# Attention and feed-forward in one kernel: w3 turned on TensorE as 32-bit words of two fp16 neighbours

## The chip, the cores and the metric

The kernel runs on one core of one Trainium2 chip. The metric is device time in microseconds (us) for one execution. The kernel before takes 422.37 us, the median of three runs (421.72 to 423.1).

## What is computed

The reference is attention with pooled queries, followed by a feed-forward block without an activation function:

```python
# q, k, v: (8, 8, 1152, 64); w1, w2: (512, 1024); w3: (1024, 1024); w_out: (1024, 512)
q_pool = q.reshape(B, H, S // 2, 2, D).mean(axis=3)          # 576 queries a head
scores = q_pool @ k.T / sqrt(D)
attn   = softmax(scores)
x      = (attn @ v), heads side by side                      # 4608 x 512
h      = (x @ w1) * (x @ w2) @ w3
out    = h @ w_out                                           # 4608 x 512, float32
```

All inputs are float32 in device memory; the kernel works in fp16 and accumulates in float32.

## The kernel before, in words

**Weights.** There is nothing between w3 and w_out but two products, so the kernel first forms T = w3 @ w_out (1024 x 512, `T16`) and later multiplies by T. For that it needs w3 with its columns on the partitions. `t_groups` (L466 to 493) does this. `turn(ft)` takes 128 rows of w3 (`w3c`, fp16, cast by the load) and turns them on TensorE with eight 128x128 transposes against `ident16` into one bank of PSUM (L475); VectorE copies the bank to `w3T` (L478). `mult(ft, n0)` then adds eight matmuls up (L484), with one 128x128 block of `w3T` as weights and a block of 256 columns of w_out (`wosb`) as moving operand, and VectorE casts the result into `T16` (L487). There are 8 turns and 16 such products of eight matmuls; the order is two turns, four products, and so on. `w3T` has two buffers.

**Attention.** Heads go in pairs, 32 pairs. A pair's k and q are loaded, cast to fp16 by GpSimd (L300 to 306) and transposed: on TensorE for the first eight pairs (`transp_pe`, L328, copied by VectorE at L330), by DMA afterwards. Scores are made in groups of 512 columns for both heads (L388) into one of three PSUM buffers (`psc`), and ScalarE's exponential moves each group into a ring in SBUF (L393). An AV group (`av_pair`, L413) multiplies 128 queries' worth of the ring by v, for both heads, into one PSUM bank (`avb`); VectorE takes reciprocals (L431), scales (L439) and, after a transpose on TensorE (L446 or L448), copies the result into `xT` (L455 or L457). The next AV group writes the same bank and waits for these.

**Feed-forward.** `xT` is worked off in nine chunks of 512 tokens (`moe_groups`): 16 projection groups of four (or eight) matmuls with w1 and w2 (L506), then four output groups of eight matmuls with `T16` (L550). VectorE (ScalarE, late in the kernel) takes them out of PSUM.

**Order.** All engines work off lists written in program order; a planner (`_Plan`) decides at build time what stands between the score groups on TensorE. The work is cut into 108 visits of three score groups each. After the scores of a visit, `plan.visit` tries sequences of fills (turns, products, projections, output groups, each into the bank `mo` or, as `mot`, into one of the three `psc` buffers), AV groups and pair transposes, and takes the one with the least lost time by its own costs: `STEP` for a fill of size n (0.45 us for a turn, n = 0.5), 0.69 us for the copy behind it, and so on. The T fills are offered from visit 3 on. A chunk of the feed-forward is offered when the AV groups that it needs are done. So a changed cost or size of one fill can move all that follows.

**Loads.** GpSimd's queue (software descriptors) brings w3 in four pieces (`w3_load`), w_out, w1, w2 and the pairs' k, q and v early on; SP's queue brings others. At the start GpSimd's list is: identity, casts of pair 0, w3 piece 0 (L607), w_out (L611), casts of pair 1, loads of pair 2, v of pair 1, cast of v of pair 0, w3 piece 1, loads of pair 3.

**The end.** `rzall` holds the reciprocals of the softmax sums. After the last AV group VectorE tests that each lies in a range, counts, and a matmul sums the count over the partitions (L744 to 757). If any test failed, a general path (`_general`) computes everything again from the inputs; otherwise it is skipped.

Of the kernel before, what the change touches and what calls it, by code (L numbers as in the profile page):

```python
# [8 lines left out]
FP32 = mybir.dt.float32  # L9
FP16 = mybir.dt.float16  # L10
AF = mybir.ActivationFunctionType
ALU = mybir.AluOpType


def _make_identity(nc, ident):
    nc.gpsimd.memset(ident, 0.0)
    nc.gpsimd.affine_select(
        out=ident, in_=ident, compare_op=ALU.not_equal, fill=1.0,
        base=0, channel_multiplier=1, pattern=[[-1, ident.shape[1]]],
    )  # L20
# [101 lines left out]
class _Plan:  # L122
# [1 line left out]


    SWITCH, SLOT, AV, TURN, PAIR, SEEN = 0.09, 0.222, 0.553, 0.055, 0.76, 0.05
    STEP = {0.5: 0.45, 1: 0.866, 2: 1.73}

    def __init__(self, t):
        self.t = t  # L130
# [21 lines left out]
    def fill(self, n, at, scored):  # L152
        b = self._psc() if scored else None
        self._pe(False, max(at, (self.psc[b] if scored else self.mo) + self.SEEN), self.STEP[n])
        self.dve = max(self.dve, self.t + 0.2) + 0.69
        if scored:
            self.psc[b] = self.dve + 0.07
        else:
            self.mo = self.dve + 0.07
# [58 lines left out]
def kernel(  # L218
# [11 lines left out]
    nc = tc.nc  # L230
# [7 lines left out]
    NF = dff // 128  # L238
# [16 lines left out]
    const = ctx.enter_context(tc.tile_pool(name="const", bufs=1))  # L255
# [4 lines left out]
    fast.enter_context(tc.manual_schedule())  # L260

    ident16 = const.tile([128, 128], FP16)
    vaugs = [const.tile([128, 2, NJ, E1], FP16, name=f"vaug{i}") for i in range(NVA)]
    rzall = const.tile([128, NU, 2], FP32)
    w1sb = wpool.tile([128, NC, dff], FP16)
    w2sb = wpool.tile([128, NC, dff], FP16)
    T16 = wpool.tile([128, NF, dm], FP16)
    msb = fast.enter_context(tc.tile_pool(name="m_sb", bufs=1))
    w3c = [msb.tile([128, 4, dff], FP16, tag="g8", bufs=2, name=f"w3c{i}") for i in range(2)]
    wosb = msb.tile([128, NF, dm], FP16)  # L270
    ring = att.tile([128, 2, RING], FP16, tag="ring", bufs=1)
    avb = ps.tile([128, 512], FP32, tag="av", bufs=1)
# [8 lines left out]
    def load_kq(p, k_eng, q_eng):  # L281
        b, h0 = p // HP, 2 * (p % HP)
        kst = att.tile([128, 2, NJ * D], FP32, tag="kst")
        k_eng.dma_start(out=kst, in_=k[b, h0:h0 + 2].rearrange("u (p c) d -> p u (c d)", p=128))
        qst = att.tile([128, 2, QM * 2 * D], FP32, tag="qst")
        qtl = att.tile([QT, 2, 2 * D], FP32, tag="qtl")
        q_eng.dma_start(out=qst, in_=q[b, h0:h0 + 2, 0:QM * 256].rearrange("u (p c) d -> p u (c d)", p=128))
        q_eng.dma_start(out=qtl, in_=q[b, h0:h0 + 2, QM * 256:S].rearrange("u (p t) d -> p u (t d)", t=2))
        kq[p] = (kst, qst, qtl)
# [7 lines left out]
    def cast_kq(p):  # L297
        kst, qst, qtl = kq.pop(p)
        kq16 = kq16s[p % 2]
        nc.gpsimd.tensor_copy(out=kq16[:, 0:NJ].rearrange("p c u d -> p u c d"),  # L300
                              in_=kst.rearrange("p u (c d) -> p u c d", d=D))
        qv = qst.rearrange("p u (c t d) -> p u c t d", t=2, d=D)
        eng = nc.gpsimd
        eng.tensor_tensor(out=kq16[:, NJ:NJ + QM].rearrange("p c u d -> p u c d"),  # L304
                          in0=qv[:, :, :, 0], in1=qv[:, :, :, 1], op=ALU.add)
        eng.tensor_tensor(out=kq16[0:QT, NJ + QM], in0=qtl[:, :, 0:D], in1=qtl[:, :, D:2 * D], op=ALU.add)
        pairs[p] = kq16
# [57 lines left out]
    def first_turn(c0, c1, pt, *engs):  # L365
        kq16, kqT = kq16s[0], pairs[0][2]
        for c in range(c0, c1):
            nc.tensor.transpose(pt[:, (c - c0) * 128:(c - c0) * 128 + 128],
                                kq16[:, c].rearrange("p u d -> p (u d)"), ident16)
        w = (c1 - c0) // len(engs)  # L370
        for n, eng in enumerate(engs):
            o = n * w
            eng(out=kqT[:, c0 + o:c0 + o + w].rearrange("p c i -> p (c i)"), in_=pt[:, o * 128:(o + w) * 128])

    def turn_bank():
        return ps.tile([128, 512], FP32, tag="mo", bufs=1, name="ptf").bitcast(FP16)
# [90 lines left out]
    def t_groups():  # L467
        w3T = {}

        def turn(ft):  # L470
            def go(pt):
                w3T[ft] = msb.tile([128, NF, 128], FP16, tag="w3T", bufs=2, name="w3T")
                ph = pt.bitcast(FP16)
                for a in range(NF):
                    nc.tensor.transpose(ph[:, a * 128:a * 128 + 128],  # L475
                                        w3c[ft // 4][:, ft % 4, a * 128:a * 128 + 128], ident16)

            return 0.5, go, lambda pt: nc.vector.tensor_copy(out=w3T[ft].rearrange("p a i -> p (a i)"),  # L478
                                                             in_=pt.bitcast(FP16)), W3_AT[ft // 2]

        def mult(ft, n0):
            def go(pT):
                for a in range(NF):
                    nc.tensor.matmul(pT[:, 0:256], w3T[ft][:, a, :], wosb[:, a, n0:n0 + 256],  # L484
                                     start=(a == 0), stop=(a == NF - 1))

            return 1, go, lambda pT: nc.vector.tensor_copy(out=T16[:, ft, n0:n0 + 256], in_=pT[:, 0:256]), WO_AT  # L487

        for ft in range(0, NF, 2):
            yield turn(ft)  # L490
            yield turn(ft + 1)
            for n in range(4):
                yield mult(ft + n // 2, n % 2 * 256)
# [116 lines left out]
    def w_load(dst, src):  # L610
        nc.gpsimd.dma_start(out=dst, in_=src.rearrange("(c p) f -> p c f", p=128))  # L611
# [11 lines left out]
    first_casts()  # L623
    rest_casts()
    w3_load(0)
    w_load(wosb, moe_w_out)
    cast_kq(1)
    load_kq(2, nc.gpsimd, nc.gpsimd)
    load_v(1, nc.gpsimd)
    cast_v(0)  # L630
# [50 lines left out]
            ready.append(held.pop(0)[1])  # L681

    NVIS = NS // VS
    seen, due, started = -1, 0.0, False
    for vis in range(NVIS):
        if vis == T_START:
            queue.append(t_groups())
        due = max(due + PACE, plan.t + 2.6)
        for s in range(vis * VS, vis * VS + VS):
            pn = (s * G + G - 1) // FLAT  # L690
            if pn != seen:
                seen = pn
                if pn == 0:
                    first_turn(0, K0, turn_bank(), nc.scalar.copy)
                    first_turn(NJ, NJ + QM, avb.bitcast(FP16), nc.vector.tensor_copy, nc.scalar.copy)
                if NPE <= pn + 1 < NP:
                    transp(pn + 1)
                if 0 < pn < NP - 2:
                    prepare(pn + 2)
                elif pn + 2 == NP:  # L700
                    cast_v(NP - 1)
            scores(s)
            plan.scores()
            if s == 0:
                first_turn(NB - 1, NB, turn_bank(), nc.vector.tensor_copy)
        if vis == 0:
            first_turn(K0, NJ, turn_bank(), nc.vector.tensor_copy)
            prepare(2)
        avail = NT5 * sum(1 for e in pair_end if e < vis) - avn[0]
        turn = [p for p in range(1, NPE) if (p * FLAT // G) // VS - 1 == vis]  # L710
        while ready:
            started = True
            queue.append(moe_groups(ready.pop(0)))
        head(4)

        must = sum(1 for i in range(avn[0], min(avn[0] + avail, NU))
                   if ((i // NT5 * NJ * Sq + RING + TO[i % NT5]) // G) // VS <= vis + 1)
        for what in plan.visit(due, [on_pe(avn[0] + j - 1) for j in range(avail)], must, [(g[0], g[3]) for g in ahead],
                               [KQ_AT.get(p, 0.0) for p in turn], 0.05 if started else 0.1):
            if what == "P":  # L720
                plan.pair(KQ_AT.get(turn[0], 0.0))
                transp_pe(turn.pop(0))
            elif what == "A":
                av_step()
                plan.av_group(on_pe(avn[0] - 2))
            else:
                fill(what == "s")
# [18 lines left out]
    nc.vector.tensor_tensor(out=ok[:, 0, :], in0=ok[:, 0, :], in1=ok[:, 1, :], op=ALU.mult)  # L746
    okn = const.tile([128, 1], FP32)
    nc.vector.reduce_sum(out=okn, in_=ok[:, 0, :], axis=mybir.AxisListType.X)
    okh = const.tile([128, 1], FP16)
    nc.vector.tensor_copy(out=okh, in_=okn)  # L750
    ones = const.tile([128, 1], FP16)
    nc.vector.memset(ones, 1.0)
    for _ in range(12):
        fill()
    nc.tensor.matmul(avb[0:1, 0:1], okh, ones, start=True, stop=True)
    badi = const.tile([1, 1], mybir.dt.int32)
    nc.vector.tensor_scalar(out=badi, in0=avb[0:1, 0:1], scalar1=-1.0, scalar2=float(128 * NQ),
                            op0=ALU.mult, op1=ALU.add)
    while not near[0]:
        fill()  # L760
    bad = nc.values_load(badi[0:1, 0:1], min_val=0, max_val=128 * NQ)
    while fill():
        pass
    fast.close()
# [32 lines left out]
```

## Time and profile before

| | |
|---|---|
| median of three runs | 422.37 us (421.72 to 423.1) |
| the profiled execution, its own time | 421.38 us |
| its span, first to last instruction | 419.4 us |
| TensorE busy | 406.3 us, 97% of the span |
| ScalarE busy | 326.4 us, 78% |
| VectorE busy | 204.8 us, 49% |
| GpSimd busy | 165.7 us, 40% |
| turns of w3 (L475) | 64 transposes, first at 18.1 us, last at 55.7 us |
| copies of the turns (L478) | 8, 0.69 us each |
| products (L484) | 128 matmuls, first at 21.4 us, last at 65.6 us |
| load of w_out | issued at 8.6 us, landed 11.2 us later |

In the profile, PE is TensorE's matmul (PEld its weight loads, which overlap), DVE is VectorE, ACT ScalarE, POOL GpSimd, SP SyncE. L475 is line 475 of the kernel before. A name like `mo<-ident,w3c` is output and inputs. Matmuls are pipelined: an instruction's duration is longer than its share of the engine, so what one costs is read from the distance between two starts.

### The profile page before, as it was taken

What the parts mean: (1) busy time and instruction counts of PE and PEld (TensorE: products, weight loads), DVE (VectorE), ACT (ScalarE), POOL (GpSimd) and SP (SyncE); (2) the same over time, 40 slices, a digit from 0 to 9 for tenths busy, and PEclk for the clock granted to TensorE, in tenths of its full rate; (3) what the DMA queues carried; (4) which work ended last, traced back from release to release, by engine and by line L of the source; (5) the groups of instructions that cost most, each with busy time, mean ns of one, the idle gap of its engine ahead of it and who ended that gap; (6) DMA issues with size and microseconds to landing.
All of it is one profiled execution on the core that took longest, in us unless ns stands there. A gap on an engine that the chain in (4) does not pass through costs nothing.

```text
span 419.4 us, 12782 instructions
## 1 busy us (share of the span) xinstructions
PE 406.3 (97%) x5337; PEld 253.2 (60%) x5337; DVE 204.8 (49%) x601; ACT 326.4 (78%) x359; POOL 165.7 (40%) x206
## 2 busy tenths in 40 slices
PE   4899999999999999999999999999999999999995
PEld 2588786566565656665566656666577756444442
DVE  1255666655355545455355534554454546624231
ACT  4888979899899989998899889999899882223231
POOL 5889967360573317250664318340642011000000
PEclk9999999999999999999999999999999999999999
DMA  8999999999798898999979999998896214020203
GB/s 273 265 305 294 287 299 325 279 264 199 188 253 208 234 262 223 272 279 265 251 195 262 253 240 291 209 266 227 225 217 120 56 64 64 14 101 2 100 0 106
DMA packets 90960, 86.34 MB, mean 206 GB/s; under 512 B 59664, under 2 KB 64272, under 8 KB 90896
## 3 DMA queue, kind: packets, MB, share of 16 engines
q1 hardware_dynamic: 81600, 59.32, 58.0%
q0 software_dynamic: 8720, 25.10, 20.6%
q10 hardware_dynamic: 576, 1.05, 0.8%
q8 instruction: 42, 0.69, 0.7%
q14 instruction: 22, 0.18, 0.2%
HBM read 67.11 MB, written 9.44 MB: 183 GB/s over the span
## 4 chain that ended last, share of the span: by engine, by line
PE 94%; ACT 2%; DVE 1%; DMA 1%; issue 1%; POOL 0%; ACTq 0%; POOLq 0%
PE avb L413 22%; PE psc L388 20%; PE mot L506 15%; PE mo L506 15%; PE mo L550 10%; PE mot L550 5%; PE mo L484 3%; ACT ring L393 2%; PE ptk L328 2%; DMA kst<-in_k_dram 1%; PE mot L484 1%; PE mot L475 1%; PE mo L475 1%; DVE kqT L330 1%; PE mol L568 0%
## 5 line engine op out<-in xcount | busy, mean ns | idle before, releaser
L393 ACT ACTIVATE ring<-psc 128x1024 f16<-128x1024 f32 x324 | 308.1, 1025 | 34.4 <-PE psc L388 32.6
L413 PEld LDWEIGHTS <-ring 128*128 128x128 f16 x2880 | 103.6, 98 | 32.1 <-issue 10.4
L413 PE MATMUL avb<-vaug,ring 128*128 128x65 f16 x2880 | 114.4, 193 | 0.1
L388 PE MATMUL psc<-kqT 64*128 64x512 f16 (+7 forms) x1152 | 96.7, 290 | 3.2 <-ACT ring L393 1.0
L388 PEld LDWEIGHTS <-kqT 64*128 64x128 f16 x1152 | 45.6, 95 | 35.0 <-issue 12.3
L300 POOL CAST kq<-kst 128x1152 f16<-128x1152 f32 x31 | 35.7, 1151 | 73.5 <-DMA kqT<-kq 52.6
L431 DVE RECIPROCAL rzall<-avb 128x2 f32<-128x2 f32 x160 | 26.3, 164 | 55.8 <-PE avb L413 26.3
L550 PE MATMUL mo<-T,gT 128*128 128x512 f16 x192 | 45.5, 380 | 0.0
L506 PEld LDWEIGHTS <-w2sb 128*128 128x128 f16 x320 | 28.4, 97 | 26.6 <-issue 2.1
L518 POOL DMA_DIRECT2D out_dram<-osb x21 | 11.7, 555 | 81.0 <-DVE osb L560 45.1
L550 PEld LDWEIGHTS <-gT 128*128 128x128 f16 x280 | 25.5, 98 | 30.1 <-issue 2.9
L506 PEld LDWEIGHTS <-w1sb 128*128 128x128 f16 x320 | 27.9, 97 | 26.0 <-issue 3.6
L313 POOL CAST vaug<-vst 128x1152 f16<-128x1152 f32 x32 | 36.6, 1143 | 8.8 <-DMA vst<-in_v_dram 8.8
L304 POOL TENSOR_TENSOR kq<-qst 128x512 f16<-128x512 f32 x31 | 39.4, 1272 | 1.5 <-DMA qst<-in_q_dram 1.5
L506 PE MATMUL mot<-xT,w2sb 128*128 128x512 f16 x156 | 40.0, 379 | 0.0
L506 PE MATMUL mo<-xT,w1sb 128*128 128x512 f16 (+2 forms) x168 | 39.2, 359 | 0.0
L539 DVE TENSOR_TENSOR gT<-mot,asb 128x512 f16<-128x512 f32 x39 | 26.9, 691 | 23.6 <-PE mot L506 23.6
L535 DVE COPY asb<-mo 128x512 f32<-128x512 f32 x38 | 26.3, 691 | 23.8 <-PE mo L506 23.8
L560 DVE TENSOR_SCALAR osb<-mo 128x512 f32<-128x512 f32 x24 | 16.6, 691 | 39.2 <-PE mo L550 39.2
L533 ACT COPY asb<-mot 128x512 f32<-128x512 f32 x20 | 11.7, 585 | 30.4 <-PE mot L506 30.4
L506 PE MATMUL mot<-xT,w1sb 128*128 128x512 f16 (+2 forms) x152 | 34.9, 356 | 0.0
L506 PE MATMUL mo<-xT,w2sb 128*128 128x512 f16 (+2 forms) x164 | 34.0, 338 | 0.0
(69 smaller groups left out, 275.8 us busy)
## 6 DMA issues: line engine op xcount, KB each, us to landing
vst<-in_v_dram SPq DMA_DIRECT2D x25, 576.0 KB, 4.8
kst<-in_k_dram SPq DMA_DIRECT2D x23, 576.0 KB, 5.7
qst<-in_q_dram SPq DMA_DIRECT2D x23, 512.0 KB, 7.3
out_dram<-osb POOLq DMA_DIRECT2D x21, 256.0 KB, 5.9
kst<-in_k_dram POOLq DMA_DIRECT2D x8, 576.0 KB, 9.5
qst<-in_q_dram POOLq DMA_DIRECT2D x8, 512.0 KB, 10.5
vst<-in_v_dram POOLq DMA_DIRECT2D x7, 576.0 KB, 6.3
out_dram<-osb SPq DMA_DIRECT2D x9, 256.0 KB, 2.0
```

The source lines that it names most:

```text
L300: nc.gpsimd.tensor_copy(out=kq16[:, 0:NJ].rearrange("p c u d -> p u c d"), in_=kst.rearrange("p u (c d) -> p u c d", d=D))
L304: eng.tensor_tensor(out=kq16[:, NJ:NJ + QM].rearrange("p c u d -> p u c d"), in0=qv[:, :, :, 0], in1=qv[:, :, :, 1], op=ALU.add)
L313: nc.gpsimd.tensor_copy(out=va[:, :, :, 0:D], in_=vs.pop(p).rearrange("p u (c d) -> p u c d", d=D))
L388: nc.tensor.matmul(psc[:, u, f - s * G:f - s * G + ln], kT2[u * 64:u * 64 + 64, jt, :], qpT[u * 64:u * 64 + 64, i0:i0 + ln], start=True, s ...
L393: nc.scalar.activation(out=ring[:, :, r0:r0 + G], in_=psc, func=AF.Exp, bias=0.0, scale=SCALE)
L413: nc.tensor.matmul(avb[:, o + u * E1:o + u * E1 + E1], ring[:, u, c0:c0 + 128], va[:, u, jt, :], start=(jt == 0 and u == 0), stop=(jt == N ...
L431: nc.vector.reciprocal(out=rzall[:, i, :], in_=av[:, :, D:E1].rearrange("p u o -> p (u o)"))
L484: nc.tensor.matmul(pT[:, 0:256], w3T[ft][:, a, :], wosb[:, a, n0:n0 + 256], start=(a == 0), stop=(a == NF - 1))
L506: nc.tensor.matmul(pw[:, d0:d0 + n], wt[:, mc, ft * 128:ft * 128 + 128], xT[:, mc, a:a + n], start=(mc == 0 and d0 == 0), stop=(mc == NC - ...
L535: nc.vector.tensor_copy(out=t["a"], in_=pa)
L539: nc.vector.tensor_tensor(out=t["g"][:, ft, :], in0=pb, in1=t["a"], op=ALU.mult)
L550: nc.tensor.matmul(po, t["g"][:, ft, tt:tt + 128], T16[:, ft, :], start=(ft == 0), stop=(ft == NF - 1))
```

## The change

Two neighbouring fp16 values of w3 are read as one word of 32 bits. A turn is then four transposes of 128x128 words against a 32-bit identity (`ident32`) in place of eight of fp16. After it, a partition holds a pair of neighbouring columns of w3, their values alternating along the row. So the weights of a product are read with a step of two elements, and w_out is loaded so that rows 2p and 2p+1 of each block of 256 lie on partition p.

`ident32` is made by GpSimd after the casts of pair 1. A new `word_test` follows the second visit's scores: VectorE fills 128x128 words with 1.0 in the lower and 0 in the upper half, TensorE turns them, VectorE copies them back and sums the lower halves (`okw`). The sum is added to the count that decides on the general path. The planner gets a fill of size 0.25 with a cost of 0.235 us in place of size 0.5 with 0.45; the copy's cost of 0.69 stays.

```diff
-    STEP = {0.5: 0.45, 1: 0.866, 2: 1.73}
+    STEP = {0.25: 0.235, 1: 0.866, 2: 1.73}
+    COPY = {0.25: 0.69, 1: 0.69, 2: 0.69}
...
+    ident32 = const.tile([128, 128], FP32)
+    okw = const.tile([128, 1], FP32)
...
-                w3T[ft] = msb.tile([128, NF, 128], FP16, tag="w3T", bufs=2, name="w3T")
-                ph = pt.bitcast(FP16)
-                for a in range(NF):
-                    nc.tensor.transpose(ph[:, a * 128:a * 128 + 128],
-                                        w3c[ft // 4][:, ft % 4, a * 128:a * 128 + 128], ident16)
-
-            return 0.5, go, lambda pt: nc.vector.tensor_copy(out=w3T[ft].rearrange("p a i -> p (a i)"),
-                                                             in_=pt.bitcast(FP16)), W3_AT[ft // 2]
+                w3T[ft] = msb.tile([128, NF * 128], FP16, tag="w3T", bufs=2, name="w3T")
+
+                w32 = w3c[ft // 4].bitcast(FP32)
+                for a in range(NF // 2):
+                    nc.tensor.transpose(pt[:, a * 128:a * 128 + 128], w32[:, ft % 4, a * 128:a * 128 + 128], ident32)
+
+            return 0.25, go, lambda pt: nc.vector.tensor_copy(out=w3T[ft], in_=pt.bitcast(FP16)), W3_AT[ft // 2]
...
+                wv = w3T[ft].rearrange("p (a i e) -> p a e i", i=128, e=2)
                 for a in range(NF):
-                    nc.tensor.matmul(pT[:, 0:256], w3T[ft][:, a, :], wosb[:, a, n0:n0 + 256],
+                    nc.tensor.matmul(pT[:, 0:256], wv[:, a // 2, a % 2, :], wosb[:, a, n0:n0 + 256],
                                      start=(a == 0), stop=(a == NF - 1))
...
-    w_load(wosb, moe_w_out)
+
+    nc.gpsimd.dma_start(out=wosb.rearrange("p (a e) n -> p a e n", e=2),
+                        in_=moe_w_out.rearrange("(a p e) n -> p a e n", p=128, e=2))
     cast_kq(1)
+    _make_identity(nc, ident32)
...
+    def word_test():
+
+        pt = turn_bank()
+        w = xT[:, 0, 0:256]
+        nc.vector.memset(w.rearrange("p (i e) -> p i e", e=2)[:, :, 0], 1.0)
+        nc.vector.memset(w.rearrange("p (i e) -> p i e", e=2)[:, :, 1], 0.0)
+        nc.tensor.transpose(pt[:, 0:256].bitcast(FP32), w.bitcast(FP32), ident32)
+        nc.vector.tensor_copy(out=w, in_=pt[:, 0:256])
+        nc.vector.reduce_sum(out=okw, in_=w.rearrange("p (i e) -> p e i", e=2)[:, 0], axis=mybir.AxisListType.X)
+
...
+        if vis == 1:
+            word_test()
...
+    nc.vector.tensor_tensor(out=okn, in0=okn, in1=okw, op=ALU.add)
```

More of the change, by code (lines that the diff above doesn't have):

```diff
@@ L154, in fill @@
         self._pe(False, max(at, (self.psc[b] if scored else self.mo) + self.SEEN), self.STEP[n])
-        self.dve = max(self.dve, self.t + 0.2) + 0.69
+        self.dve = max(self.dve, self.t + 0.2) + self.COPY[n]
         if scored:
@@ L756 @@
     badi = const.tile([1, 1], mybir.dt.int32)
-    nc.vector.tensor_scalar(out=badi, in0=avb[0:1, 0:1], scalar1=-1.0, scalar2=float(128 * NQ),
+    nc.vector.tensor_scalar(out=badi, in0=avb[0:1, 0:1], scalar1=-1.0, scalar2=float(128 * (NQ + 128)),
                             op0=ALU.mult, op1=ALU.add)
@@ L760 @@
         fill()
-    bad = nc.values_load(badi[0:1, 0:1], min_val=0, max_val=128 * NQ)
+    bad = nc.values_load(badi[0:1, 0:1], min_val=0, max_val=128 * (NQ + 128))
     while fill():
```

## The prediction

> **What bounds the kernel now.** I read the page first (busy shares, chain), then the timeline of all engines over the first 30 us, TensorE's timeline over the stage that the change touches (30 to 75 us), and VectorE's beside it. A time with a difference of 0.3% (1.27 us here) is what a measurement of this kernel can tell from no change.
>
> From the page:
>
> ```profile
> PE 406.3 (97%) x5337; PEld 253.2 (60%) x5337; DVE 204.8 (49%) x601; ACT 326.4 (78%) x359; POOL 165.7 (40%) x206
> ...
> PE 94%; ACT 2%; DVE 1%; DMA 1%; issue 1%; POOL 0%; ACTq 0%; POOLq 0%
> ```
>
> TensorE is busy for 97% of the span and makes 94% of the chain that ended last. All its listed waits together come to 8.4 us, nearly all before 28 us. So from there on a microsecond taken from TensorE's work is a microsecond off the end, if the order written by the planner gives it other work; before that, ScalarE, transfers and VectorE hold it up.
>
> TensorE's timeline (start us, us, then the group):
>
> ```profile
> 31.74 0.61 PE L475 MATMUL mot<-ident,w3c 128*128 128x128 f16 x8
> 32.19 0.61 PE L475 MATMUL mo<-ident,w3c 128*128 128x128 f16 x8
> 32.63 0.71 PE L413 MATMUL avb<-vaug,ring 128*128 128x65 f16 x18
> 34.12 1.05 PE L484 MATMUL mo<-wosb,w3T 128*128 128x256 f16 x8
> 35.00 1.04 PE L484 MATMUL mot<-wosb,w3T 128*128 128x256 f16 x8
> ...
> 62.78 0.71 PE L413 MATMUL avb<-vaug,ring 128*128 128x65 f16 x18
> ...
> 64.26 0.72 PE L413 MATMUL avb<-vaug,ring 128*128 128x65 f16 x18
> ```
>
> What counts is start to start: a turn of eight takes 0.45 (31.74 to 32.19), 56 ns a transpose; a product of eight takes 0.88, 110 ns each.
>
> The timeline of all engines, early:
>
> ```profile
> 10.78 5.61 ACT L393 ACTIVATE ring<-psc 128x1024 f16<-128x1024 f32 x6 [0.35 <-PE psc L388]
> ...
> 11.85 0.61 PE L388 MATMUL psc<-kqT 64*128 64x384 f16 x4 [0.27 <-ACT ring L393]
> ...
> 11.85 0.46 POOL L306 TENSOR_TENSOR kq<-qtl 64x128 f16<-64x128 f32 x1
> ...
> 18.14 1.04 PE L475 MATMUL mot<-ident,w3c 128*128 128x128 f16 x8
> 18.97 1.06 PE L475 MATMUL mo<-ident,w3c 128*128 128x128 f16 x8
> ...
> 20.35 0.62 POOL L288 DMA_DIRECT2D qtl<-in_q_dram  x1 [2.00 <-DMA wosb<-in_moe_w_out_dram]
> ...
> 24.40 0.44 POOL L306 TENSOR_TENSOR kq<-qtl 64x128 f16<-64x128 f32 x1
> ...
> 25.19 0.94 PE L328 MATMUL ptk<-ident,kq 128*128 128x128 f16 x14
> ```
>
> The first two turns take 0.83 and 0.99: up to 19.8 us the transposes start 107 ns apart, after that 56. The granted clock in the rows is 1.00 all along, so it does not show this; the durations do.
>
> **1. The turns (L475).** 64 transposes of 128x128 with 64 weight loads become 32 of words. Nothing of 32 bits on TensorE is in the trace, so the price of one is bounded: 56 ns if it streams its 128 columns as an fp16 one does, 98 if its load (98 ns mean in the L475 load row) no longer hides, 224 if each needs four passes. I take 56, the same instruction on the same 128 columns. Then a turn takes 4 x 0.056 = 0.22 instead of 0.45. Six turns lie after 30 us: 6 x 0.22 = 1.3 us of TensorE. The first two are at the slow pace: 4 x 0.107 = 0.43 each instead of 0.83 and 0.99, 0.96 less, but only part of it lasts (3). The evicting copy (L478, 0.69) is unchanged. Its cover shrinks: in two visits the new order is turn, AV group, turn, product, so 0.60 + 0.22 = 0.8 us lie before the product that reads the first copy, just enough for its 0.69 and the 0.1 that a copy starts after the turn; uncovered, some 0.1 twice.
>
> The TensorE page of the Trainium skill (Terms) calls transpose mode four times faster for FP32, and the FP8 and floating point page (TensorE Precision Notes) gives FP32 four passes. By the first a word costs what I took, by the second my four-pass end; no run here shows either yet.
>
> **2. The products (L484).** 128 of them now load weights with a step of two elements. Every load in the trace has step one and takes 95 to 99 ns inside the 110 ns of its matmul, which streams 256 columns. If stepped loads keep within 110, cost nothing; if a load were no longer hidden at all, 128 x 98 ns = 12.5 us. I take nothing: the load has the matmul as its cover, and the pace of the turns (a pair each 56 ns) shows that loads of 98 ns overlap each other by almost half, so they may double before they show.
>
> The TensorE page (weight-path modes) allows fast loads "packed or strided" with steps up to 1,024, but not for FP32; by that rule the products stay at 110 ns a matmul and a word's load is of the slow kind; no row here shows a slow load.
>
> **3. The early stage.** The new identity costs GpSimd a memset and a select between L306's end (12.3) and the load at 12.25: by the fp16 ones (0.21 and 0.29) 0.5 us, at most 1.0 if words cost double. Queued behind are four load issues, the cast of v and two more loads; the next stop of GpSimd is the 2.00 us wait at 18.35 for w_out, which swallows it. The loads themselves sit in a transfer queue that is full (in the trace's packet records those of w3 and w_out run without a break from 10 to 18.9 us), so a later issue does not land later. w_out arrives as 512 packets instead of 1,024: packets of 2 KB took 174 ns each, of 1 KB 98, so 512 x 174 / 16 = 5.6 instead of 6.3 us, 0.7 sooner, for k and q of pair 2 too.
>
> The word test (one transpose) stands on TensorE behind the sixth score group and waits for that identity, so to 12.8 to 13.3. Behind it, in order, is the seventh score group, which ran at 11.85 to 12.46 and now ends about 13.7 to 14.2. ScalarE wants it at 13.59 (third of the six at 10.78, 0.935 each). So ScalarE, and TensorE behind it (three score buffers), slip 0.1 to 0.6; I take 0.2. VectorE is idle there for 6 us, and the test's memsets, copy and sum cost nothing.
>
> The two turns then save 0.96 while ScalarE is 0.2 late; the next score groups wait for its buffers. The group after the turns could start at 19.3, but its second half needs the buffer of the exponential that ended at 19.77, now 19.97; so TensorE comes out at 20.55 where it was at 20.86. That is 0.3 earlier. The transposes of pair 2 (25.19) wait for GpSimd's cast that ends at 24.84, tight; with w_out's 0.7 us it ends near 24.1, so 0.3 passes. Bounds: -0.2 to 0.96.
>
> **4. The order.** The planner's lists, compared, differ only in visits 2 to 32; from visit 33 (114.2 us before) to the end they are the same. The freed time lets the projections begin one visit sooner (visit 17 for 18), so the first chunk runs out one visit sooner: visits 28 to 32 were A-p-A, o-A, o-A, o-A, o-A (A an AV group, p a projection group, o an output group), and become o-A four times and then A-A, two AV groups with only a transpose of x between. The second chunk is not ready yet. VectorE's timeline shows what lies between two AV groups:
>
> ```profile
> 63.58 0.17 DVE L431 RECIPROCAL rzall<-avb 128x2 f32<-128x2 f32 x1 [0.18 <-PE avb L446]
> 63.78 0.29 DVE L439 TENSOR_TENSOR xbt<-avb,rzall 128x128 f16<-128x128 f32 x1
> 63.99 0.21 DVE L455 COPY xT<-avb 128x128 f16<-128x128 f16 x1
> ```
>
> The AV group at 62.78 frees its bank at 64.20, and the next starts at 64.26: 1.48 us, in which TensorE has 0.60 of its own here. So 0.88 us of the gain is idled away. The visit then takes 2.9, and ScalarE's three exponentials 2.86, so it cannot shrink anyway. Bounds: 0.4 to 0.9.
>
> **5. The end.** One more VectorE addition near 360.8 us (a small operation like L750's 0.16) before a matmul at 371.36: ten microseconds of cover.
>
> **Sum.** -0.3 (early) - 1.3 (six turns) + 0.9 (visit 32) = -0.7 us. The profiled execution took 421.38 (span 419.4), 0.99 below the median 422.37; from its rows it becomes 420.7, on the median's scale **421.7**.
>
> **Rivals.**
> - *The gain is kept whole*: the early saving stays (0.96) and the hole in visit 32 costs 0.4. -0.96 - 1.3 + 0.4 = -1.9: 420.5 on the median's scale, as all that follow. For it: w_out sooner, GpSimd's slack. Against: ScalarE's buffers at 19.97 and the 1.48 us chain.
> - *The word's load sets the pace*, 98 ns: six turns save only 6 x (0.45 - 0.39) = 0.4. -0.3 - 0.4 + 0.9 = +0.2: 422.6.
> - *Four passes* (slower): 0.89 a turn, +0.44 x 6 = 2.7; the first two 1.71 each, +1.6; word test 0.2; hole 0.9: +5.4, 427.8. It is slower from about 130 ns a word on. For it: an operand twice as wide, and no row.
> - *Full pace comes later.* It came at about 20 us, after TensorE had worked without a gap from 17.2; turns half as long leave a gap at 19.6. If it comes one such stretch (2.8 us) later, half of it, 1.4 us, is added: -0.7 + 1.4 = +0.7, 423.1. The TensorE page (Part 1) names a free-running window of 3.4 us after which the clock is released; by it this would be 423.4, and the trace's single change of pace neither bears out nor denies the length.
> - *The words are not carried whole*: the test sends words whose upper half is zero; if these come out as zero, the flag is set and the general path follows: 64 heads x 6 steps, each with a DMA transpose of at least 1.5 us (fastest such row): over 576 us more.
>
> **Chances.** Forecast 55 (21 of it faster by over 0.3%, 33 within, 1 slower), kept whole 17 (faster), load pace 8 (6 within, 2 slower), four passes 9, late clock 8 (6 within, 2 slower), words not carried 3. Faster 21 + 17 = 38, within 33 + 6 + 6 = 45, slower 1 + 2 + 9 + 2 + 3 = 17. The range 420.2 to 423.6 takes in the bounds of 3 and 4, the load pace and the late clock, and leaves out four passes, lost words and some of the tails; the forecast alone has 420.7 to 422.7.
>
> **What would show it.** Starts of the word transposes 56 ns apart (98 or 224 for the rivals); products still 0.88 a group; the seventh score group ending near 13.7 and ScalarE idle 0.2 there; the transposes of pair 2 near 24.9; an idle stretch of 0.9 on TensorE in visit 32, at about 112 us; visit 33 some 0.7 earlier than 114.2, and the same distance to the end. I am wrong if visit 33 moves by over 1.3 us either way, or if it moves as said and the end does not.

## The result, and the profile after

The changed kernel takes **422.54 us** (median, 421.95 to 424.44), the kernel before, on the same chip, 421.8 (421.16 to 423.1). The ratio is 1.0023 with a 95% interval from 1.0012 to 1.0033: **0.5 to 1.4 us slower, about 1.0**. (The medians are 0.74 apart and the means 0.96, because 7 of 20 executions of the changed kernel lie above 423 us and 1 of 20 of the one before.) 421.7 and 0.7 us faster had been forecast. The profiled execution took 422.68 (span 420.9), 1.3 more than that of before. Lines of the changed kernel are numbered three higher than before from L388 on (scores L391, exponential L396, AV groups L416), and four higher in the turns (L479); products are L487. A *stretch* below is the time between two marks in one trace.

The page after, busy shares and chain:

```profile
PE 405.7 (96%) x5306; PEld 252.5 (60%) x5306; DVE 206.0 (49%) x606; ACT 326.4 (78%) x359; POOL 166.2 (39%) x208
PE 93%; DMA 1%; ACT 1%; POOL 1%; issue 1%; DVE 1%; SPq 0%; POOLq 0%; ACTq 0%
```

31 matmuls fewer (32 in the turns, one more in the word test), and yet TensorE's busy time hardly falls, while its share of the chain falls from 94 to 93% and POOL's rises to 1%. So little was saved, and something new is waited for.

TensorE's timeline of the changed kernel (start, us, group; in brackets the idle time before it and what ended it):

```profile
13.82 0.47 PE L696 MATMUL ptf<-ident,xT 128*128 128x128 f32 x1 [1.93 <-POOL ident L17]
...
15.95 1.53 PE L331 MATMUL ptk<-ident,kq 128*128 128x128 f16 x14 [0.26 <-ACT ring L396]
...
19.11 0.66 PE L479 MATMUL mot<-ident,w3c 128*128 128x128 f32 x4
19.61 0.60 PE L479 MATMUL mo<-ident,w3c 128*128 128x128 f32 x4
20.14 1.11 PE L391 MATMUL psc<-kqT 64*128 64x192 f16 x12
...
25.57 0.94 PE L331 MATMUL ptk<-ident,kq 128*128 128x128 f16 x14
...
31.37 0.66 PE L479 MATMUL mo<-ident,w3c 128*128 128x128 f32 x4
31.87 0.71 PE L416 MATMUL avb<-vaug,ring 128*128 128x65 f16 x18
...
32.45 0.63 PE L479 MATMUL mot<-ident,w3c 128*128 128x128 f32 x4
32.92 1.04 PE L487 MATMUL mo<-wosb,w3T 128*128 128x256 f16 x8
```

Three things. *A turn of four words takes as long as one of eight fp16 blocks*: 31.37 to 31.87 is 0.50, 32.45 to 32.92 is 0.47, where 0.45 was taken before (0.47 to 0.54 over all eight). *The word test* (L696) waits 1.93 for `ident32`, the 32-bit identity that GpSimd makes. *The pair-2 transposes* start at 25.57 (25.19 before).

The groups of the changed kernel (busy us, mean ns of one, idle before), the weight loads of the turns into `mot` and those of the products:

```profile
L479 PEld LDWEIGHTS mot<-ident,w3c 128*128 128x128 f32 x16 | 1.7, 141 | 0.3 <-ACT ring L396 0.2
...
L487 PEld LDWEIGHTS <-w3T 128*128 128x128 f16 x128 | 11.8, 98 | 2.3 <-issue 1.1
```

The load of a word block takes 141 ns where that of an fp16 block took 98; the products' load, now with a step of two, is still 98.

TensorE around visit 32 in the kernel before, where an output group (L550) stands ahead of the AV group:

```profile
111.85 1.90 PE L550 MATMUL mo<-T,gT 128*128 128x512 f16 x8
113.59 0.71 PE L413 MATMUL avb<-vaug,ring 128*128 128x65 f16 x18
114.23 0.82 PE L388 MATMUL psc<-kqT 64*128 64x512 f16 x10
```

All engines around visit 32 of the changed kernel:

```profile
113.48 0.72 PE L416 MATMUL avb<-vaug,ring 128*128 128x65 f16 x18
...
114.05 0.19 PE L451 MATMUL avb<-ident,xbt 128*128 128x64 f16 x1
...
114.27 0.17 DVE L434 RECIPROCAL rzall<-avb 128x2 f32<-128x2 f32 x1 [0.84 <-PE avb L451]
114.48 0.29 DVE L442 TENSOR_TENSOR xb<-avb,rzall 128x128 f16<-128x128 f32 x1
114.69 0.21 DVE L460 CAST xT<-avb 128x64 f16<-128x64 f32 x1
114.95 0.71 PE L416 MATMUL avb<-vaug,ring 128*128 128x65 f16 x18 [0.71 <-DVE xT L460]
115.59 0.90 PE L391 MATMUL psc<-kqT 64*128 64x512 f16 x10
```

Here are the two AV groups with only a transpose of x between, and the wait on TensorE before the second: 0.90 from the start of that transpose to the next start, 0.71 of it listed as idle. Visit 33 starts at 115.59, 1.36 after 114.23 in before; from there to the last AV group the two traces run alike within 0.1.

**Where it came from.** I cut both traces at five marks.

| stretch (us) | before | after | difference |
|---|---|---|---|
| start to the first score group | 6.70 | 7.00 | +0.30 |
| to the transposes of pair 2 | 18.50 | 18.57 | +0.07 |
| to the 71st AV group | 145.88 | 146.90 | +1.02 |
| to the last AV group | 185.80 | 185.81 | 0 |
| to the last output group | 56.03 | 56.13 | +0.10 |

The first row is the landing of an input load, ahead of all that changed. What is left: the middle stretch, the tail, and an early stage whose balance needs explaining, since the test lost 1.9 us there.

### The profile page after: what moved, and what is told of

It reads as the page before. It is cut to its first block, busy times and chain, and to the rows that moved or that the text cites. A ratio compares the mean times of both kernels' runs of the same rounds, so it can differ in the third digit from the quotient of the medians.

```text
span 420.9 us, 12725 instructions
## 1 busy us (share of the span) xinstructions
PE 405.7 (96%) x5306; PEld 252.5 (60%) x5306; DVE 206.0 (49%) x606; ACT 326.4 (78%) x359; POOL 166.2 (39%) x208
## 4 chain that ended last, share of the span: by engine, by line
PE 93%; DMA 1%; ACT 1%; POOL 1%; issue 1%; DVE 1%; SPq 0%; POOLq 0%; ACTq 0%
PE avb L416 22%; PE psc L391 20%; PE mot L509 15%; PE mo L509 15%; PE mo L553 10%; PE mot L553 5%; PE mo L487 3%; PE ptk L331 2%; DMA kst<-in_k_dram 1%; ACT ring L396 1%; PE mot L487 1%; DVE kqT L333 1%; PE mot L479 1%; PE mo L479 0%; PE mol L571 0%
## 5 line engine op out<-in xcount | busy, mean ns | idle before, releaser
L396 ACT ACTIVATE ring<-psc 128x1024 f16<-128x1024 f32 x324 | 308.1, 1025 | 35.5 <-PE psc L391 33.7
L416 PEld LDWEIGHTS <-ring 128*128 128x128 f16 x2880 | 103.9, 98 | 32.7 <-issue 11.3
L416 PE MATMUL avb<-vaug,ring 128*128 128x65 f16 x2880 | 114.4, 194 | 0.8 <-DVE xT L460 0.7
L391 PE MATMUL psc<-kqT 64*128 64x512 f16 (+7 forms) x1152 | 96.3, 289 | 2.5 <-ACT kqT L376 0.8
L391 PEld LDWEIGHTS <-kqT 64*128 64x128 f16 x1152 | 45.3, 95 | 33.8 <-issue 11.7
L509 PE MATMUL mot<-xT,w2sb 128*128 128x512 f16 x148 | 38.0, 379 | 0.0
L509 PE MATMUL mo<-xT,w1sb 128*128 128x512 f16 (+2 forms) x160 | 37.1, 358 | 0.0
L509 PE MATMUL mot<-xT,w1sb 128*128 128x512 f16 (+2 forms) x160 | 37.0, 358 | 0.0
L542 DVE TENSOR_TENSOR gT<-mot,asb 128x512 f16<-128x512 f32 x37 | 25.5, 691 | 23.4 <-PE mot L509 23.4
L509 PE MATMUL mo<-xT,w2sb 128*128 128x512 f16 (+2 forms) x172 | 36.1, 340 | 0.0
L542 DVE TENSOR_TENSOR gT<-mo,asb 128x512 f16<-128x512 f32 x35 | 24.2, 692 | 22.3 <-PE mo L509 22.3
```

Source lines behind the costliest of these rows:

```text
L391: nc.tensor.matmul(psc[:, u, f - s * G:f - s * G + ln], kT2[u * 64:u * 64 + 64, jt, :], qpT[u * 64:u * 64 + 64, i0:i0 + ln], start=True, s ...
L396: nc.scalar.activation(out=ring[:, :, r0:r0 + G], in_=psc, func=AF.Exp, bias=0.0, scale=SCALE)
L416: nc.tensor.matmul(avb[:, o + u * E1:o + u * E1 + E1], ring[:, u, c0:c0 + 128], va[:, u, jt, :], start=(jt == 0 and u == 0), stop=(jt == N ...
L509: nc.tensor.matmul(pw[:, d0:d0 + n], wt[:, mc, ft * 128:ft * 128 + 128], xT[:, mc, a:a + n], start=(mc == 0 and d0 == 0), stop=(mc == NC - ...
L542: nc.vector.tensor_tensor(out=t["g"][:, ft, :], in0=pb, in1=t["a"], op=ALU.mult)
```

## The experiments

Two theories on a word were left by the trace: **A1**, its moving columns stream at half the rate of fp16; **A2**, its longer load (141 ns) no longer hides. And three places for the loss: the order (the hole of visit 32), the late identity in front of the word test, and the words themselves. Each kernel is one of before and after with some of these put back. "Old order" below means that every engine's list is that of before, but for the word test where it is kept.

**Paces by themselves.** Behind the last output group of a kernel with words, the old order and an early identity (below), rows of 24 matmuls are added; nothing is left out:

```diff
+    row("ua", lambda pt, j: nc.tensor.transpose(pt.bitcast(FP16)[:, 0:128], u16[:, j * 128:j * 128 + 128], ident16))
+    row("ub", lambda pt, j: nc.tensor.transpose(pt[:, 0:128], u32[:, j * 128:j * 128 + 128], ident32))
+    row("uc", lambda pt, j: nc.tensor.transpose(pt[0:64, 0:128], u32[:, j * 128:j * 128 + 64], ident32))
+    row("ud", lambda pt, j: nc.tensor.transpose(pt[:, 0:64], u32[0:64, j * 128:j * 128 + 128], ident32[0:64, 0:64]))
...
+    row("ue", prod(1, 64))
+    row("uf", prod(2, 64))
+    row("ug", prod(8, 64))
...
+    row("uj", prod(1, 256))
+    row("uk", prod(2, 256))
```

`uc` loads 64 columns as weights instead of 128, `ud` streams 64 columns of the identity instead of 128 (and has half the rows); `prod(step, n)` loads weights with that step and streams n columns.

> The changed kernel with the order of before and the early identity, and behind its last matmul eleven rows of 24 TensorE instructions of one kind back to back, which add about 25 us and nothing to the output. ua fp16 transposes 128x128; ub words 128x128; uc words with 64 columns loaded; ud words of 64 rows against an identity of 64; ue, uf, ug products of 64 moving columns with weights of step 1, 2, 8; uh, ui of 128 columns with step 1, 2; uj, uk of 256 columns with step 1, 2. Theory A1 (a word's 128 columns stream at half rate): ua 56, ub 109, uc 109, ud 56 ns from start to start. Theory A2 (the load of 32-bit weights sets the pace): ua 56, ub 109, uc about 60, ud 109. For stepped loads: if they are as fast as plain ones, uf and ug equal ue, ui equals uh, uk equals uj at 109; if a step halves the load's rate, uf is slower than ue, and uk still 109.

TensorE's timeline of this kernel (one execution), the added rows:

```profile
414.96 1.50 PE L799 MATMUL ua<-ident,w1sb 128*128 128x128 f16 x24
416.30 2.79 PE L800 MATMUL ub<-ident,w1sb 128*128 128x128 f32 x24
418.93 2.78 PE L801 MATMUL uc<-ident,w1sb 128*64 128x128 f32 x24
421.64 1.71 PE L802 MATMUL ud<-ident,w1sb 64*128 64x64 f32 x24
423.28 0.87 PE L796 MATMUL ue<-T,w1sb 128*128 128x64 f16 x24
423.99 0.86 PE L796 MATMUL uf<-T,w1sb 128*128 128x64 f16 x24
424.69 1.66 PE L796 MATMUL ug<-T,w1sb 128*128 128x64 f16 x24
...
428.86 2.78 PE L796 MATMUL uj<-T,w1sb 128*128 128x256 f16 x24
431.48 2.78 PE L796 MATMUL uk<-T,w1sb 128*128 128x256 f16 x24
```

From start to start within a row: fp16 transposes 56 ns, words 109 (`ub`). With half the loaded columns the load falls from 142 to 111 ns, and the distance stays 109 (`uc`); with half the streamed columns and half the rows it falls to 62 (`ud`), though the load there still takes 139. **A2 falls, and A1 fits**: a word costs what its 128 columns take at half rate, which is two fp16 transposes (112) within 3 ns. Columns and rows were not halved apart, so that it is the columns is read from `ub` and `uc` and not shown by itself. Weights with a step of two cost nothing, at 64 columns (29 and 29 ns) as at 256 (109 and 109); a step of eight does (62 at 64 columns, its loads mostly 163 to 177 ns instead of 98).

**The order alone.** The kernel before, with fp16 turns, told to the planner at the price of word turns, so that it writes the changed kernel's order:

```diff
-    STEP = {0.5: 0.45, 1: 0.866, 2: 1.73}
+    STEP = {0.5: 0.235, 1: 0.866, 2: 1.73}
```

> The kernel before with the planner told 0.235 us for a turn: fp16 transposes, no word test, no stepped loads, but the order of the changed kernel. Theory A: the idle stretch of 0.9 us in visit 32 alone, so 0.9 us slower than before (ratio 1.002). Theory B: as before (ratio 1.000).

422.13 against 421.52, ratio 1.0013 (1.0004 to 1.0022). TensorE's timeline of it around visit 32:

```profile
113.47 0.72 PE L413 MATMUL avb<-vaug,ring 128*128 128x65 f16 x18
...
114.94 0.71 PE L413 MATMUL avb<-vaug,ring 128*128 128x65 f16 x18 [0.72 <-DVE xT L457]
```

The same hole with no word in the kernel. From the transposes of pair 2 to the 71st AV group it takes 146.78, 0.90 more than before. The planner's price makes this loss, not the instruction.

**The old order with words.** The changed kernel with a price of 0.45 for a turn:

```diff
-    STEP = {0.25: 0.235, 1: 0.866, 2: 1.73}
+    STEP = {0.25: 0.45, 1: 0.866, 2: 1.73}
```

> The changed kernel with the planner told 0.45 us for a turn again, so that its order on TensorE is that of the kernel before, with the word test added. Theory A (a word costs 109 ns at any pace, so six turns save nothing, and the loss is the idle stretch of 0.9 us between two AV groups of visit 32 that the new order makes): the stretch is gone, 0.9 us off the changed kernel, within 0.4 us of the kernel before. Theory B (the loss sits in the word test and in the stepped loads, the order is harmless): no change against the changed kernel, +0.7 us against before.

421.8 against 421.52, 1.0015 (0.9999 to 1.0031): by itself undecided. The trace decides the stretch. TensorE's timeline of it at the same place:

```profile
112.79 1.90 PE L553 MATMUL mo<-T,gT 128*128 128x512 f16 x8
114.53 0.71 PE L416 MATMUL avb<-vaug,ring 128*128 128x65 f16 x18
115.17 0.83 PE L391 MATMUL psc<-kqT 64*128 64x512 f16 x10
```

An output group stands ahead of the AV group, and there is no wait. The stretch to the 71st AV group is 145.96, and 145.95 to 145.97 in the three other kernels with this order and six word turns; with this order and six fp16 turns it is 145.88 to 145.90 in all six traces. In the new order it is 146.90 to 146.92 with words, in three traces, and 146.78 without. So six word turns cost 0.05 to 0.14 us, about 0.1, and gain nothing.

**A pause that looks like an effect.** Between the 76th and the 77th AV group VectorE stands still for 0.28 us in some of the kernels. VectorE's timeline of the kernel before, then of the old order with words:

```profile
180.84 0.17 DVE L431 RECIPROCAL rzall<-avb 128x2 f32<-128x2 f32 x1 [0.90 <-PE avb L448]
181.28 0.29 DVE L439 TENSOR_TENSOR xb<-avb,rzall 128x128 f16<-128x128 f32 x1 [0.28 <-DVE rzall L431]
```

```profile
181.77 0.17 DVE L434 RECIPROCAL rzall<-avb 128x2 f32<-128x2 f32 x1 [0.90 <-PE avb L451]
181.97 0.29 DVE L442 TENSOR_TENSOR xb<-avb,rzall 128x128 f16<-128x128 f32 x1
```

The next AV group waits for the copy behind this scaling and comes 0.25 later. The pause is in the traces of the kernel before, of the changed one (both times), and of the early identity, the stepped fp16 turns and the two warmed kernels below; it is missing in the other seven, the old order with words and the new order alone among them. The traces name no cause. So a kernel without it is 0.25 us better off against the kernel before, for a reason that is not its edit's; the result itself, with the pause on both sides, does not contain it. That is why the stretches here end at the 71st AV group.

**The identity early.** `_make_identity(nc, ident32)` moved ahead of the first casts, the rest as changed:

> The changed kernel with the 32-bit identity made right behind the fp16 one, ahead of the casts of pair 0. Theory A: the word test no longer waits, the transposes of pair 1 start about 1.0 us sooner than in the changed kernel, and 0.3 to 0.8 us of it arrive at the end (ScalarE's three buffers and the cast of pair 2 may keep the rest). Rival: GpSimd's later casts of pair 0 delay the first scores by the 0.5 us of the identity, and nothing is gained.

422.7 against 421.52, 1.0033 (1.0021 to 1.0044): a miss, nothing was gained. TensorE's timeline of it:

```profile
11.59 0.47 PE L696 MATMUL ptf<-ident,xT 128*128 128x128 f32 x1
...
14.67 1.65 PE L331 MATMUL ptk<-ident,kq 128*128 128x128 f16 x14 [0.31 <-ACT ring L396]
...
18.22 1.11 PE L479 MATMUL mot<-ident,w3c 128*128 128x128 f32 x4
19.12 1.06 PE L479 MATMUL mo<-ident,w3c 128*128 128x128 f32 x4
20.11 1.46 PE L391 MATMUL psc<-kqT 64*128 64x192 f16 x12
...
26.38 0.83 PE L331 MATMUL ptk<-ident,kq 128*128 128x128 f16 x12
```

The edit did what it should: the test no longer waits, and the transposes of pair 1 are 1.3 earlier than in the changed kernel. Yet the transposes of pair 2 come at 26.38. In this execution TensorE still runs at half pace (starts twice as far apart) at 20: its turns take 0.90 and 0.99, its score group of twelve 1.40. What had been gained by then was lost to the slow pace. So I looked at when full pace comes, in every trace (where distances from start to start fall to half):

| kernel | full pace at | first score group to pair 2 | pair 2 to 71st AV group |
|---|---|---|---|
| before | 20.2 | 18.50 | 145.88 |
| after | 17.2 | 18.57 | 146.90 |
| old order | 21.3 | 19.17 | 145.96 |
| new order alone | 21.0 | 18.87 | 146.78 |
| early identity | 22.6 | 19.62 | 146.92 |

It comes anywhere from 17 to 23 us, and where it comes later than in the kernel before, the transposes of pair 2 move by about half a us for each us of it. That is a scatter of the single execution, greater than what I look for in this stage. So the next kernels each have one early cause, and are judged by their medians and by the time at a given moment of full pace.

**Stepped fp16 turns, w_out in 512 packets, no words and no test.** Kernel before, old order; the transposes read every second fp16 value:

```diff
-                                        w3c[ft // 4][:, ft % 4, a * 128:a * 128 + 128], ident16)
+                                        w3c[ft // 4][:, ft % 4].rearrange("p (a i e) -> p a e i", i=128, e=2)[:, a // 2, a % 2],
+                                        ident16)
...
-    w_load(wosb, moe_w_out)
+    nc.gpsimd.dma_start(out=wosb.rearrange("p (a e) n -> p a e n", e=2),
+                        in_=moe_w_out.rearrange("(a p e) n -> p a e n", p=128, e=2))
```

> The kernel before with w_out loaded in row pairs and w3 turned by eight fp16 transposes that take every second column (stepped loads), so no words and no word test; order of before. Theory A: stepped loads are free, w_out lands 0.7 us sooner, and nothing at that time waits for it: as before within 0.3 us (ratio 1.000). Rival: w_out and the loads behind it are what TensorE waits for at the transposes of pair 2, and 0.3 us are won.

422.08 against 421.99, 1.0006 (0.9998 to 1.0015). The load of w_out gains nothing that shows.

**The same with the word test and the late identity** (`ident32`, `word_test` and `okw` put back, turns fp16):

> The kernel of e5 with the changed kernel's word test and its identity behind the casts of pair 1; the turns stay fp16. What the word test costs alone. Theory A: its wait delays the transposes of pair 1 by 0.5 to 1.3 us, but half or more of that is lost again in waits for ScalarE and the slow pace of that stage, so 0.2 to 0.6 us slower than before. Rival: the tail of slow executions of the changed kernel (7 of 20 above 423) comes from the test, then this one has it too.

422.36, 1.0010 (0.9998 to 1.0021). The test ran at 13.40; the transposes of pair 1 were 0.9 later after the first score group, those of pair 2 0.4 to 0.5 later than its moment of full pace (21.5) lets expect. At the end it added 0.10.

**Words only in the first two turns, and words only in the last six** (old order, early identity; the others are stepped fp16 transposes):

```diff
+                if ft >= 2:
+                    w16 = w3c[ft // 4][:, ft % 4].rearrange("p (a i e) -> p a e i", i=128, e=2)
+                    ph = pt.bitcast(FP16)
+                    for a in range(NF):
+                        nc.tensor.transpose(ph[:, a * 128:a * 128 + 128], w16[:, a // 2, a % 2], ident16)
+                    return
```

(`ft < 2` in the second kernel.)

> Words for the first two turns only, the other six by stepped fp16 transposes; identity early, order of before. Theory A: a word costs two fp16 transposes at the slow pace too (219 ns against 107), so the first two turns are as long as before, and the whole is as before within 0.3 us. Rival: words count less for whatever releases TensorE's full pace, the release comes later in some executions, and the tail above 423 us appears here.

> The reverse: stepped fp16 for the first two turns, words for the six behind them; identity early, order of before. Theory A: six turns of 0.47 in place of 0.45: 0.1 us slower than before, no tail. Rival: as e7 if the tail comes from something else than the words.

422.54, 1.0008 (0.9996 to 1.0021), and 422.23, 1.0010 (1.0001 to 1.0019), against 421.99. Neither place of the words has a loss of its own that shows beside the stepped fp16 kernel's 1.0006, and neither a gain. In the first, the two turns run at half pace and take 0.91 and 0.99 (0.83 and 0.99 before): also there a word is worth two.

**A try for an earlier full pace.** Matmuls on `ident16` into an unused bank give TensorE more work from the start, once with the kernel before and once with the stepped fp16 kernel:

```diff
+                    warm(7, 512)
                     first_turn(0, K0, turn_bank(), nc.scalar.copy)
...
             scores(s)
+            if 3 <= s < 8:
+                warm(1, 256)
```

> The kernel before with extra matmuls that compute nothing: seven of 512 columns on TensorE ahead of the first transposes (it waits there for input until 4.8 us) and one of 256 behind each of the score groups 4 to 8. Tests what the early stage owes to TensorE's slow pace, which ended anywhere from 17.2 to 22.6 us in the profiles so far. If activity releases the full pace, it comes before 16 us here, the time from the first score group to the transposes of pair 2 falls from 18.5 to 19.6 to about 18.2 (where the cast of pair 2 holds it), and 0.5 us is won on the median. If the pace depends on something else, the extra work costs up to 0.5 us or nothing.

> e9 with the load of w_out in row pairs and the stepped fp16 transposes of e5. If w_out's shorter transfer lets the cast of pair 2 end 0.7 us sooner, the time from the first score group to the transposes of pair 2 falls below that of e9, to about 17.6, and the median is up to 1 us below the kernel before. If something else holds that stage, as e9.

422.25 against 421.63, 1.0013 (1.0004 to 1.0021), and 422.43, 1.0021 (1.0007 to 1.0035): another miss. TensorE's timeline of the first:

```profile
18.96 0.62 PE L481 MATMUL mot<-ident,w3c 128*128 128x128 f16 x8
19.42 0.61 PE L481 MATMUL mo<-ident,w3c 128*128 128x128 f16 x8
```

Full pace did not come before 16 us, as it was to if activity alone released it, but at 17.3, no sooner than in the changed kernel without the extra work; so this does not show what releases it. The first turn took 0.46, but each warming matmul takes 0.33 ahead of its score group. So the transposes of pair 1 come 0.4 later after the first score group, and those of pair 2 18.18 after it (18.07 in the second kernel, with full pace about as early), 0.3 less than before. Below some 18.1 it did not get in any trace, which I put down to ScalarE's exponentials; that was argued, not tried.

**Words with old order and early identity**, all that was found undone but the words, the test and the load:

> The changed kernel with both losses taken away: the order of before (no idle stretch in visit 32) and the early identity (the word test does not wait). Theory A: what is left is 0.1 us for six word turns and 0.1 us at the end, so 0.2 us over the kernel before (ratio 1.0005, not over 1.0015 at the middle), and 1.1 us below the changed kernel of e12. Theory B (the loss lies in the words or the stepped loads): as e12.

422.66 against 422.12, 1.0007 (0.9994 to 1.0020), beside **the changed kernel once more** on the same chip:

> The changed kernel on the same chip as e11. Theory A: 0.9 us for the idle stretch, 0.2 to 0.5 for the word test's wait, 0.2 as in e11: 1.3 to 1.6 us over the kernel before (ratio 1.003 to 1.004); by the first measurement alone 1.0023.

423.02, 1.0021 (1.0008 to 1.0035): the result repeats. The kernel with old order and early identity was to lie 1.1 below this one; by the medians it lies 0.4 below. TensorE's timeline of this one:

```profile
14.38 0.47 PE L696 MATMUL ptf<-ident,xT 128*128 128x128 f32 x1 [2.13 <-POOL ident L17]
...
27.48 0.94 PE L331 MATMUL ptk<-ident,kq 128*128 128x128 f16 x14
```

Full pace came at 22.7 here, and the transposes of pair 2 two us later than in the first profile of the same kernel. No kernel of the study beats the one before.

## Why the prediction was wrong

**The step that failed is step 1, the term "6 x 0.22 = 1.3 us of TensorE".** I took 56 ns for a word, "the same instruction on the same 128 columns". The instruction and the columns are the same, but a word starts 109 ns after the one before, so four of them take as long as eight fp16 blocks: a turn took 0.47 to 0.54 where it had taken 0.45. So the term is about +0.1 (by the stretch to the 71st AV group), not -1.3, and the rest of the forecast was a sum of losses that this gain was to pay for. The prediction's own sign of being wrong came with it: visit 33 moved by +1.36 instead of by -0.7.

The Trainium skill's page TensorE: Matmul & The Clock Gate (Terms) calls transpose mode four times faster for FP32. The trace agrees in part: 109 ns is far below the 224 of four passes, but it is two fp16 transposes and not one; the measurement decides.

**Rivals.** The number of "the word's load sets the pace", 422.6, was nearly right and its mechanism wrong: the load is off the path, as the half load showed. That its 98 ns lay near 109 is chance. Four passes did not come; nor did lost words, as the general path did not run.

**Full pace later**: in the profile after it came 3 us sooner than before, in the second one 2.5 later. Two executions of one kernel are 5.5 us apart in it, so these traces put no part of the result down to it. They do not rule it out either: few executions were traced, and the one of 424.71 us, with full pace at 22.7, lost 1.6 us more than the first one ahead of the transposes of pair 2. Whether the changed kernel's other long executions are of this kind is not shown.

**Step 2, products**: right. 0.87 and 0.88 from start to start, load 98 ns; the step of two is free.

**Step 4, the hole of 0.9 in visit 32**: right, in place and size (0.90 from the transpose of x to the next start, 0.71 of it listed as idle), and in cause: the order alone has it, and its stretch to the 71st AV group is 0.90 longer.

**Step 3, early**: the identity cost 0.5 of GpSimd as said (rows 0.22 and 0.29 below). What I had too early is when it starts in this execution. GpSimd in the changed kernel:

```profile
13.18 0.22 POOL L16 MEMSET ident<- 128x128 f32 x1
13.47 0.29 POOL L17 TENSOR_SCALAR_AFFINE_SELECT ident<-ident 128x128 f32<-128x128 f32 x1
...
20.43 0.62 POOL L291 DMA_DIRECT2D qtl<-in_q_dram  x1 [0.62 <-DMA wosb<-in_moe_w_out_dram]
```

The test went at 13.82, not at 12.8 to 13.3, and the transposes of pair 1 at 15.95 instead of 14.60. GpSimd was late already: its second cast of k, which waits for a load, went at 8.04 instead of 6.96. In the other three executions with a late identity the test went at 12.95, 13.40 and 14.38, so the forecast was within the scatter. The later wait for w_out did swallow the GpSimd time, 2.00 shrank to 0.62. But the saving that was to follow from shorter turns was not there, and the two early turns at full pace (0.50 and 0.53) are the work of this execution's early full pace. Executions without the test whose full pace came as early or earlier than 19.2 us have 18.1 to 18.2 from the first score group to pair 2; this one, with full pace at 17.2, has 18.57, so 0.4 of the delay is left there. By the same reading against before (half a us for each us of full pace) 0.1, 0.5 and 0.4 are left in the other three executions with a late identity; the six kernels without one whose full pace came later than before's lie 0 to 0.2 below this reading. That is a reading of single executions: the medians with and without the test (1.0010 and 1.0006) cannot tell it from nothing. I had -0.3.

**Step 5, "ten microseconds of cover"**: off by 0.1. The addition delays VectorE there (its timeline, then TensorE's, in the changed kernel):

```profile
362.27 0.16 DVE L767 TENSOR_TENSOR okn<-okn,okw 128x1 f32<-128x1 f32 x1
```

```profile
362.31 1.03 PE L509 MATMUL mot<-xT,w1sb 128*128 128x512 f16 x4
363.28 0.59 PE L509 MATMUL mot<-xT,w2sb 128*128 128x512 f16 x2
```

One projection group waits for its buffer: 0.97 to the next start instead of 0.86. I asked who waits for the sum, and not who waits for VectorE. All kernels with the test have a tail of 56.13, all without 56.03.

**The sum again**: +0.1 (six turns) + 0.9 (hole) + 0.1 (tail) + 0 to 0.5 (early) = 1.1 to 1.6, measured 0.5 to 1.4. The ratios divide it less sharply: the five kernels with the old order and words or the test have 1.0007 to 1.0015 (mean 1.0010) and lack VectorE's pause, the three with the new order and words 1.0021, 1.0023 and 1.0033 (mean 1.0026) and have it, the new order alone 1.0013, without it. With the pause taken into account the order is worth 0.4 us by the first pair and 0.8 by the last figure, where the traces have 0.9; each ratio's interval is about 0.4 us to either side, or more. And the five with the old order are 0.4 us slower than the kernel before, though their word turns (0.1) and tail (0.1) are no more than the missing pause (0.25). What makes these 0.4 us is not resolved; the early stage, which scatters, is where the traces leave room for it.

**Open**: why full pace comes when it does, how much of the test's early delay reaches the median, and why VectorE pauses in some kernels and not in others.

## What to carry to other kernels

Fewer instructions were not less time on TensorE here: half as many transposes, each at half the rate, took the same. So an operand twice as wide has to be priced by a row of its own, and where there is none, the forecast should rest on bounds and not on "the same instruction". A price told to a planner moves work far from the edit; a wrong one (0.235 for a turn of 0.47) bought a hole of 0.9 us at a place where nothing had been changed. When a small operation is put on an engine with slack, look for who waits behind it on that engine, at the end of the kernel too. And a stretch that is compared between kernels should be cut fine enough that a pause which is not the change's shows by itself.

## What the runs showed of the hardware that was not expected

- A transpose of 128 words of 32 bits starts 109 ns after the one before at full pace and 213 to 214 at half pace, an fp16 one 56 and 107. With 64 columns and 64 rows a word transpose takes 62 and not 55. The load of a word block takes 141 ns (98 for fp16) and stays hidden.
- Weights read with a step of two load as fast as packed ones (98 ns); with a step of eight they mostly take 163 to 177, and products of 64 columns start 62 ns apart where 29 was the pace.
- The pace of TensorE doubles once, at a moment that lies between 17.2 and 22.8 us from one execution to another, though the granted clock reads 1.00 throughout. It goes with shifts of up to a microsecond in this kernel's early stage and is part of why single executions differ.
